# A transformer block on one Trainium2 core: weight bounds from sums on ScalarE, filler products on TensorE, a planner with longer transfer estimates, and part of h transposed by DMA

## The chip, the cores and the metric

The kernel runs on one core of one Trainium2 chip. Its engines are TensorE (PE in the profile, its weight loads PEld), VectorE (DVE), ScalarE (ACT), GpSimd (POOL) and SyncE (SP), which here only issues transfers; a second queue of transfers is issued by ScalarE (ACTq). The metric is the device time of one execution in microseconds. The kernel before takes 1078.31 us, the median of three runs (1075.23 to 1079.66).

## The reference

```python
B, S, D = 1, 2048, 640;  H = 32; Dh = 20; W = 256;  F = 1536
qkv = layernorm(x) @ wqkv                                # no scale or shift in the norm
scores = einsum("bhqd,bhkd->bhqk", q, k) * Dh ** -0.5
mask = (i - j >= 0) & (i - j < W)                        # a sliding window of 256 keys
o = softmax(where(mask, scores, -1e9)) @ v
h = x + o @ wo
h2 = h + (gelu(layernorm(h) @ w_gate) * (layernorm(h) @ w_up)) @ w_down
```

All inputs and the output are 32-bit floats.

## The kernel before

**Tiles.** The 2048 rows are 16 blocks of 128. q and k are made for chunks of two blocks (`qk`, eight chunks), v for one block (`vproj`), the feed-forward for chunks of four blocks (`gate_up`, `down`, four chunks of three weight groups each). Every dense product is made of three 16-bit products: each operand is split into a high half (`...h`) and a low half (`...l`), and hi*hi, hi*lo and lo*hi are summed in a PSUM bank. So 75 matmuls of 256 columns make q (or k) of a chunk.

**Weights.** `Weight.scale` finds a power of two that brings a weight into range: DVE takes the largest absolute value of each of its five slices of 128x640 (tile `am`), a small product with a diagonal (`dg`) spreads it over the partitions, and a few short DVE operations make the scale `sw`. `Weight.split` then makes the high half on ACT and the low half on DVE. The weights are numbered in the profile: w0 is q's, w1 k's, w2 v's, w3 that of the output product, gu and w5 to w9 gate and up, w10 to w12 down.

**Attention.** For each block and each pair of heads there are two short row-tiled products, each on two halves of the array at once: `maxima` (q times k, whose row maxima DVE takes in `max_out`, tile `junk`) and, once a block's maxima have gone through `max_rows` and a transfer into two spare rows of qT, `scores` (k times q, exponentiated by ACT in `score_out` into `pt`, masked by GpSimd). Four score tiles make a unit, which `value_lane` multiplies with v (tile `pv`). q and k reach their stacked layout through DRAM: `qk_out` writes 16-bit halves from the ACT queue and `stack` reads them back with six transfers each from the SP queue into `qT` and `kT`.

**Layer norms.** `layernorm` normalises a block on DVE (tile `lxn` for h) with one power on GpSimd, and `transpose_part` transposes it on TensorE in two pieces of four and one 128x128 tiles into the bank `tp`; ACT casts the high half out of PSUM and DVE subtracts the low half. The first chunk of h is normalised during attention (`first_norm_lane`), the other three are read back from DRAM in the feed-forward (`chunk_lane`, `norm_lane`, tiles `hTh` and `hTl`).

**What sets the order.** The program is written out by a planner. Each task is a generator (a lane) that says for which engine and operands it waits; class `Clock` keeps an estimated time of every engine and operand, and the loop at the end takes the first lane in a list of priorities that its estimate lets start now. What comes out is a fixed order on each engine. On the chip an engine carries out its row in that order, and waits only for semaphores. `row_need` chooses whether the two banks of `ra` and `rb` hold a maxima and a scores pair next; `Lane.start` holds the allowances.

The names and lines that the prediction speaks of are `Clock.issue` (158), `Weight.scale` (352) and `split` (387), `layernorm` (422), `stack` (664), `maxima` (719), `row_need` (739), `scores` (823), `norm_lane` (1064) and `big_lane` (543).

## Time and profile before

| | |
|---|---|
| median of three runs | 1078.31 us (1075.23 to 1079.66) |
| profiled execution, its own time | 1078.47 us |
| profiled execution, span | 1076.6 us |
| TensorE busy | 1031.5 us (96%) |
| VectorE, ScalarE, GpSimd busy | 673.8, 456.8, 182.8 us |
| mean granted TensorE clock | 0.994 |

The profile's page shows a single execution. The busy time of TensorE counts a matmul from its start to its modelled end, so successive matmuls overlap in it; what a matmul costs is the distance to the start of the next one. In the timeline, each row has a start, the time from the first start to the last end of the merged instructions, the engine, the operation, out<-in, shapes and a count; what stands in brackets is the time that the engine sat idle before it and what ended that. Nearly every instruction is recorded in a helper and so has the line L188: groups are told apart by their tiles. DMA issues on SP and ACT are rows of SPq and ACTq, and last as long as the issue, not the transfer.

### The profile page before, as it was taken

How to read it: one execution, taken by the hardware profiler on the slowest of the kernel's cores; microseconds unless marked ns; L12 is line 12 of the kernel's file. 1: busy time of each engine (PE TensorE's matmuls, PEld its weight loads, DVE VectorE, ACT ScalarE, POOL GpSimd, SP SyncE). 2: the span in 40 equal slices, each digit the busy share in tenths (PEclk: the TensorE clock that was granted, in tenths of full speed). 3: DMA queues.
4: the chain of work that ended last, by engine and by line, in shares of the span. 5: the costliest groups of instructions: out<-in, count | busy, mean ns of one | idle time of the engine just before them, and what ended most of it. 6: DMA issues, size and time to landing. Idle time of an engine off the chain costs nothing.

```text
span 1076.6 us, 25043 instructions
## 1 busy us (share of the span) xinstructions
PE 1031.5 (96%) x10122; PEld 632.3 (59%) x10122; DVE 673.8 (63%) x1993; ACT 456.8 (42%) x904; POOL 182.8 (17%) x297
## 2 busy tenths in 40 slices
PE   4888899999999999999999999999999999999998
PEld 2645566666776666676655564555555555545546
DVE  7967799888778777776789379724522262212323
ACT  2414466665676666665667744310211121110110
POOL 5001113232333333332333300000000000000000
PEclk9989999999999999999999999999999999999999
DMA  7536436214142230414142034002000020001001
GB/s 280 124 93 161 141 108 169 85 58 116 38 113 63 74 88 30 105 57 98 32 173 65 13 122 147 2 1 98 1 1 1 25 74 1 1 1 50 1 1 49
DMA packets 63251, 76.91 MB, mean 71 GB/s; under 512 B 6112, under 2 KB 42208, under 8 KB 62176
## 3 DMA queue, kind: packets, MB, share of 16 engines
q1 hardware_dynamic: 40032, 64.57, 20.2%
q10 hardware_dynamic: 23104, 10.75, 3.7%
q8 instruction: 79, 1.29, 0.5%
q14 instruction: 36, 0.29, 0.1%
HBM read 54.07 MB, written 20.97 MB: 70 GB/s over the span
## 4 chain that ended last, share of the span: by engine, by line
PE 82%; DVE 8%; DMA 3%; ACT 3%; issue 2%; ACTq 1%; POOL 0%; SPq 0%; DVEq 0%; POOLq 0%
PE mm L188 62%; PE pv L188 7%; PE tp L188 4%; PE ra L188 4%; PE rb L188 4%; DVE junk L188 2%; ACT pt L188 2%; DVE am L188 1%; DMA qk<-qks 1%; DMA kT<-qk 1%; ACTq L188 1%; DMA wsl<-in_wo_dram 1%; DVE m L188 1%; DMA qT<-in_wqkv_dram 1%; DMA xt<-in_x_dram 1%
## 5 line engine op out<-in xcount | busy, mean ns | idle before, releaser
L188 POOL TENSOR_SCALAR_AFFINE_SELECT pt<-pt 128x512 f32<-128x512 f32 x240 | 151.0, 652 | 371.6 <-ACT pt L188 371.6
L188 ACT ACTIVATE pt<-ra,esc 128x384 f32<-128x384 f32 (+2 forms) x262 | 133.0, 560 | 82.9 <-PE ra L188 71.4
L188 DVE CUSTOM_DVE_ANT_0 junk<-rb,mask 128x384 bf16<-128x384 f32 (+2 forms) x260 | 138.1, 531 | 44.1 <-PE rb L188 23.4
L188 DVE CUSTOM_DVE_ANT_0 junk<-ra,mask 128x384 bf16<-128x384 f32 (+2 forms) x252 | 133.0, 528 | 43.5 <-PE ra L188 19.5
L188 ACT ACTIVATE pt<-rb,esc 128x384 f32<-128x384 f32 (+2 forms) x250 | 126.9, 561 | 71.0 <-PE rb L188 64.3
L188 DVE SCALAR_TENSOR_TENSOR gel<-mm,ffk,gel 128x512 f32<-128x512 f32 x48 | 35.9, 749 | 141.4 <-PE mm L188 141.4
L188 ACT ACTIVATE gel<-mm,ffk 128x512 f32<-128x512 f32 x48 | 33.0, 688 | 187.9 <-PE mm L188 187.8
L188 PE MATMUL pv<-pt,v 128*21 128x128 f32 x2880 | 104.3, 276 | 1.7 <-ACT oT L188 1.5
L188 DVE SCALAR_TENSOR_TENSOR ht<-mm,ffk,ht 128x320 f32<-128x320 f32 x96 | 52.8, 550 | 81.6 <-PE mm L188 81.6
L188 PEld LDWEIGHTS <-ah 128*128 128x128 f16 x768 | 75.1, 98 | 30.9 <-issue 0.4
L188 ACT CAST ah<-gel 128x512 f16<-128x512 f32 x48 | 29.8, 621 | 121.2 <-DVE gel L188 121.1
L188 PEld LDWEIGHTS pv<-pt,v 128*21 128x21 f32 x2880 | 68.6, 100 | 16.7 <-ACT oT L188 2.2
L188 PEld LDWEIGHTS <-gu 128*128 128x128 f16 x480 | 45.8, 98 | 53.0 <-issue 0.8
L188 PEld LDWEIGHTS <-kT 62*128 62x128 f16 x1440 | 59.2, 94 | 28.0 <-issue 14.2
L188 PE MATMUL mm<-hTh,gu 128*128 128x512 f16 x240 | 71.9, 379 | 0.0
L188 PEld LDWEIGHTS <-qT 60*128 60x128 f16 x640 | 26.3, 93 | 70.2 <-issue 65.2
L188 PE MATMUL mm<-xh,w1h 128*128 128x256 f16 x200 | 55.6, 278 | 3.0 <-DVE qks L188 3.0
L188 PE MATMUL mm<-xh,w0h 128*128 128x256 f16 x200 | 56.1, 280 | 1.9 <-ACT w0h L188 1.9
L188 PE MATMUL mm<-xh,w0l 128*128 128x256 f16 x200 | 55.7, 278 | 1.0 <-DVE w0l L188 1.0
L188 PE MATMUL mm<-xh,w1l 128*128 128x256 f16 x200 | 55.8, 279 | 0.2 <-DVE w1l L188 0.2
L188 PE MATMUL mm<-xl,w0h 128*128 128x256 f16 x200 | 55.9, 280 | 0.0
L188 PE MATMUL mm<-xl,w1h 128*128 128x256 f16 x200 | 55.6, 278 | 0.0
(214 smaller groups left out, 2316.2 us busy)
## 6 DMA issues: line engine op xcount, KB each, us to landing
qk<-qks ACTq DMA_DIRECT2D x64, 128.0 KB
qT<-qk SPq DMA_DIRECT2D x48, 160.0 KB
kT<-qk SPq DMA_DIRECT2D x48, 160.0 KB
ht<-in_x_dram SPq DMA_DIRECT2D x16, 320.0 KB
h_dram<-ht SPq DMA_DIRECT2D x16, 320.0 KB
ht<-h_dram SPq DMA_DIRECT2D x16, 320.0 KB
out_dram<-ht SPq DMA_DIRECT2D x15, 320.0 KB
xt<-in_x_dram SPq DMA_DIRECT2D x13, 320.0 KB
```

The source lines that it names most:

```text
L188: r = real(*args, **kw)
```

## The change

Four things are changed.

1. **Bounds from sums.** For the three weights of q, k and v, `scale` takes the sum of absolute values of each slice on ACT (an `Abs` activation with `accum_out`) in place of the largest absolute value on DVE. The sum bounds the maximum, so the power of two is larger. The output of the activation goes into the room of the high half, which is written anew by `split`.
2. **Filler products.** As long as no maxima have been issued, whenever the planner finds nothing to do and TensorE free in its estimate, it writes a product of the 16-bit identity with itself into the order (into `pv`).
3. **Planner.** A transfer is estimated to land 2.6 us (SP) or 2.2 us (other queues) after its bytes in place of 1.7, its issue to take 0.7 us where its rows are short, and its bytes 1.2 times as long. Transfers of `stack` are spaced by that estimate. Lanes marked `soon` (short links of a chain) come first. Blocks 0 and 1 put two pairs of heads into a bank (`pairs`). `row_need` may also choose two scores or two maxima pairs. The memsets of `kT` on GpSimd wait until w0 is scaled. GELU and `down` wait until their scales have been written.
4. **h of chunks 1 to 3.** `turned` casts the normalised block to a high half on ACT (tile `sph`, 128x640), subtracts the low half on DVE (`spl`), and two transposing transfers on the SP queue write them into `hTh` and `hTl`. The twelve blocks are no longer transposed on TensorE and nothing of them goes through PSUM.

The core of the diff:

```diff
@@ Clock.issue, Engine
         if move:
-            self.t[eng] = start + 0.4
-            self.moved[eng] = max(self.moved[eng], start + 0.2) + cost
-            end = self.moved[eng] + 1.7
+            run = min(b[4] for a, (_, b) in zip(reads + writes, boxes[0] + boxes[1])
+                      if a.space != DRAM)
+            self.t[eng] = start + (move if run > 512 else 0.7)
+            self.moved[eng] = max(self.moved[eng], start + 0.2) + cost * (1.2 if run <= 512 else 1)
+            end = self.moved[eng] + (2.6 if eng == "sync" else 2.2)
...
+                             {"dma_start": 0.4, "dma_start_transpose": 1.2}.get(op))
@@ Weight.scale
             for i in range(n):
+                if self.hl:
+                    yield on("scalar", self.raw[0, i])
+                    nc.scalar.activation(self.hl[0][:, i, :], self.raw[0, i], AF.Abs,
+                                         accum_out=am[:, i:i + 1])
+                    continue
@@ layernorm, after xn is made
+        if dma:
+            yield from turned(xn, lane, (hi, lo), dst, when)
+            return
...
+    def turned(src, lane, to, dst=None, when=None):
+        yield on("scalar", src, when=lambda: not opened["parts"] and (not when or when()))
+        opened["parts"] += 1
+        hi, lo = (nc.tile(ffp, [P, D], F16, n) for n in ("sph", "spl"))
+        nc.scalar.copy(hi, src)
+        yield on("vector", hi)
+        nc.vector.tensor_tensor(lo, src, hi, op=ALU.subtract)
+        if dst:
+            to = dst()
+        for o, i in zip(to, (hi, lo)):
+            yield ("sync",), need(i, eng="sync")
+            nc.sync.dma_start_transpose(o, i)
+        opened["parts"] -= 1
@@ big_lane
-                yield on("gpsimd")
+                yield on("gpsimd", when=lambda: W["q"].scaled)
@@ stack
+                if c > 1:
+                    yield ("sync",), lambda: nc.moved["sync"] - PACE
@@ pairs, used by maxima, scores, max_out and score_out
+    def pairs(j):
+        return 2 if j < 2 else 1
@@ row_need
+        late = max(ta, nc.t["tensor"]) + APART
+        two_of = [(maxima, scores, tm[:1] + ts[:1]), (scores, scores, ts), (maxima, maxima, tm)]
+        if lead > LEAD + SWAY:
+            two_of = [two_of[1], two_of[0], two_of[2]]
+        elif lead < LEAD - SWAY:
+            two_of = [two_of[2], two_of[0], two_of[1]]
+        for f, g, t in two_of:
+            if len(t) == 2 and max(tb, *t) <= late:
+                row.extend([(f, a), (g, b_)])
+                return max(tb, *t)
@@ gelu, down
-        yield on("scalar", ps)
+        yield on("scalar", ps, when=lambda: pos["ffk", fg])
...
-        yield pe(when=lambda: w.ready and pos["act", c, fg] == FT)
+        yield pe(when=lambda: w.ready and w.down and pos["act", c, fg] == FT)
@@ norm_lane
-                                 xn=lambda: nc.tile(ffp, [P, D], F32, "lxn", 2))
+                                 xn=lambda: nc.tile(ffp, [P, D], F32, "lxn", 2), dma=True)
@@ the loop at the end
+        first = [l for l in trans + sides if isinstance(l.engs, Soon)]
-        order = (early + outs + trans + sides
+        order = (first + early + outs + trans + sides
...
         else:
+            if not pos["max"] and nc.t["tensor"] <= now:
+                nc.tensor.matmul(pv[:, 0, :], ident16, ident16, start=True, stop=True)
             now += 0.03
```

How the rows of three engines move. First ScalarE at the start of the program, before: the four casts belong to the transposes of x blocks 0 and 1, `w0h<-qT,sw` is the split of q's weight, whose slices lie in the tile qT at first.

```order
L188 ACT_TABLE_LOAD
L188 CAST xh<-tp 128x4x128
L188 CAST xh<-tp 128x128
L188 CAST xh<-rb 128x4x128
L188 CAST xh<-rb 128x128
L188 ACTIVATE w0h<-qT,sw 128x640 x5
L188 ACTIVATE qks<-mm 128x512
```

And now:

```order
L190 ACT_TABLE_LOAD
L190 ACTIVATE w0h,am_159<-qT 128x640 x2
L190 CAST xh<-tp 128x4x128
L190 ACTIVATE w0h,am_159<-qT 128x640
L190 CAST xh<-rb 128x4x128
L190 ACTIVATE w0h,am_159<-qT 128x640
L190 CAST xh<-tp 128x128
L190 CAST xh<-rb 128x128
L190 ACTIVATE w0h,am_159<-qT 128x640
L190 ACTIVATE w1h,am_349<-gu 128x640 x2
L190 ACTIVATE w0h<-qT,sw 128x640 x5
```

The five sums of w0 (those with `am`) now stand on ScalarE between the casts, and the third, fourth and fifth of them stand behind casts that need TensorE's transposes.

TensorE at its first transposes, before and then now (`ident_76` is the 16-bit identity; 52 rows of the filler product stand ahead of the piece shown):

```order
L188 MATMUL tp<-ident,xt 128x128 x5
L188 MATMUL rb<-ident,pt 128x128 x4
L188 MATMUL ra<-dg,ones 128x128
L188 MATMUL rb<-ident,pt 128x128
L188 LDWEIGHTS w0h
L188 MATMUL mm<-xh,w0h 128x256
```

```order
L190 LDWEIGHTS ident_76
L190 MATMUL pv<-ident_76 128x128
L190 MATMUL tp<-ident,xt 128x128 x4
L190 LDWEIGHTS ident_76
L190 MATMUL pv<-ident_76 128x128
```

The first five transposes stood at the head of the row; now a run of filler products precedes them, and further runs (14, 7, 4 and 38 products) stand between them and the small product with `dg` that spreads the bound of w0. 247 filler products are in the program in all.

SyncE's queue from the last weight to the results of the first feed-forward chunk, before and then now:

```order
L188 DMA wst<-in_wd_dram 128x640 x4
L188 DMA ht<-h_dram 128x640 x4
L188 DMA out_dram<-ht 128x640 x4
L188 DMA ht<-h_dram 128x640 x4
```

```order
L190 DMA wst<-in_wd_dram 128x640 x4
L190 DMA ht<-h_dram 128x640 x4
L190 DMA_TRANSPOSE hTh<-sph 128x5x128
L190 DMA_TRANSPOSE hTl<-spl 128x5x128
L190 DMA_TRANSPOSE hTh<-sph 128x5x128
L190 DMA_TRANSPOSE hTl<-spl 128x5x128
L190 DMA_TRANSPOSE hTh<-sph 128x5x128
L190 DMA_TRANSPOSE hTl<-spl 128x5x128
L190 DMA_TRANSPOSE hTh<-sph 128x5x128
L190 DMA_TRANSPOSE hTl<-spl 128x5x128
L190 DMA out_dram<-ht 128x640 x4
```

Eight transposing transfers stand between the loads of a chunk of h and the stores of the chunk before it. On TensorE the 60 transposes `tp<-ident,lxn` of chunks 1 to 3 are gone (384 transposes into `tp` before, 324 now). Over the whole program TensorE goes 282 times into a run of the row-tiled products of attention before, and 252 times now.

More of the change, by code (lines that the diff above doesn't have):

```diff
@@ L156, in others, with issue @@
                             if e != eng])
-    def issue(self, eng, cost, reads, writes, move=False):
+    def issue(self, eng, cost, reads, writes, move=None):
         start = self.t[eng]
@@ L192, in call @@
                 out, ins = [aps[0], aps[-1]], aps[1:-1]
+            if "accum_out" in kw:
+                out, ins = [aps[0], aps[-1]], aps[1:-1]
             if op in ("memset", "affine_select"):
                 ins = out if op == "affine_select" else []
-            self.clock.issue(self.name, self.cost(op, out[0], ins), ins, out, op == "dma_start")
+            self.clock.issue(self.name, self.cost(op, out[0], ins), ins, out,
+                             {"dma_start": 0.4, "dma_start_transpose": 1.2}.get(op))
             return r
@@ L385, in scale, with room @@
             self.known = True
+        def room(self, pool):
+            if not self.hl:
+                self.hl = pool if isinstance(pool, tuple) else [
+                    nc.tile(pool, [P] + self.shape, F16, f"w{self.col}{x}") for x in "hl"]
         def split(self, pool, spread=0):
-            self.hl = pool if isinstance(pool, tuple) else [
-                nc.tile(pool, [P] + self.shape, F16, f"w{self.col}{x}") for x in "hl"]
+            self.room(pool)
+            self.begun = True
             sc = sw[:, self.col:self.col + 1]
@@ L682, in stack @@
             for b in (2 * c, 2 * c + 1):
-                for pr in range(H // 2):
+                for pr in range(0, H // 2, pairs(b)):
                     heapq.heappush(maxq, (b, pr))
@@ L750, in row_need @@
+        free = 3 - (pos["units"] - pos["values"])
+        for j, pr in list(scoreq)[:2]:
             b = B[j]
-            ts = nc.ready((b.c.qT[0:62, pr, b.cols], b.c.qT[64:126, pr, b.cols]), "tensor")
-            if pr % 2 == 0 and pos["units"] - pos["values"] >= 3:
-                ts = INF
+            free -= pr % 2 == 0
+            if free >= 0:
+                ts.append(nc.ready((b.c.qT[0:62, pr, b.cols], b.c.qT[64:126, pr, b.cols]),
+                                   "tensor"))
         row.clear()
-        both = tm is not None and ts is not None
@@ L756, in row_need @@
-        lead = pos["max"] - pos["score"]
-        if both and max(tb, tm, ts) > max(ta, nc.t["tensor"]) + APART:
-            both = False
-            if max(tm, ta) > max(ts, ta) + APART or lead > LEAD and ts < INF:
-                tm = None
-            else:
-                ts = None
-        if both:
-            row.extend([(maxima, a), (scores, b_)])
-            return max(tb, tm, ts)
-        if tm is not None:
-            row.append((maxima, a))
-            return max(ta, tm)
-        if ts is not None:
-            row.append((scores, a))
-            return max(ta, ts)
@@ L774, in block_kernel @@
+        one = [(max(ta, t[0]), f) for f, t in ((maxima, tm), (scores, ts)) if t]
+        if len(one) == 2:
+            (t0, _), (t1, _) = one
+            one = one[1:] if t0 > t1 + APART or lead > LEAD else one[:1]
+        if not one:
+            return INF
+        row.append((one[0][1], a))
+        return one[0][0]
     row = []
@@ L820, in max_transpose @@
         side.append((LATE, residual(j)))
-        scoreq.extend((j, pr) for pr in range(H // 2))
+        scoreq.extend((j, pr) for pr in range(0, H // 2, pairs(j)))
     def scores(at_):
@@ L1154, in dense_lane @@
                 else:
-                    yield pe(when=lambda: woq or any(can(*t) for t in list(todo)[:AHEADQ]))
+                    yield pe(when=lambda: woq and W["o", 0].ready
+                             or any(can(*t) for t in list(todo)[:AHEADQ]))
             else:
```

112 lines of the change are left out of this document (67 added, 45 removed).

## The prediction

> **What bounds the kernel now.** I read the page first, then a table of five stretches.
>
> ```profile
> span 1076.6 us, 25043 instructions
> PE 1031.5 (96%) x10122; PEld 632.3 (59%) x10122; DVE 673.8 (63%) x1993; ACT 456.8 (42%) x904; POOL 182.8 (17%) x297
> PE 82%; DVE 8%; DMA 3%; ACT 3%; issue 2%; ACTq 1%; POOL 0%; SPq 0%; DVEq 0%; POOLq 0%
> core 0: us, PE busy (x) PEld busy (x) DVE busy (x) ACT busy (x) POOL busy (x), PEclk, DMA share, GB/s
> 0.00:58.00 58.00, 33.45 (x232) 24.20 (x232) 47.73 (x123) 20.38 (x35) 17.10 (x31) 0.99 0.65 198
> 58.00:120.00 62.00, 54.26 (x454) 34.14 (x456) 45.01 (x189) 19.83 (x50) 5.57 (x9) 0.90 0.51 141
> 120.00:620.00 500.00, 490.57 (x6875) 321.56 (x6869) 394.38 (x1293) 329.46 (x676) 153.28 (x245) 1.00 0.30 83
> 620.00:1073.00 453.00, 452.98 (x2569) 252.38 (x2567) 186.13 (x388) 87.10 (x143) 6.86 (x12) 1.00 0.10 33
> ```
>
> TensorE carries 82% of the chain, but not equally. From 620 us on it never stops, so there only fewer matmuls help. From 120 to 620 us it idles 9.4 us, but pays for going to and fro between dense and row-tiled products. Up to 120 us it idles 32.3 us (24.55 and 7.74); in the second stretch the clock of 0.90 takes another 62 * 0.10 = 6.2 us. What is to be gained lies at the start, in the changes to and fro, and in the transposes of the end.
>
> **The transposes of chunks 1 to 3.** TensorE in the feed-forward:
>
> ```profile
> 753.03 0.38 PE L188 MATMUL mm<-hTh,w5l 128*128 128x512 f16 x1
> 753.25 0.60 PE L188 MATMUL tp<-ident,lxn 128*128 128x128 f32 x4
> 753.69 0.38 PE L188 MATMUL mm<-hTh,w5h 128*128 128x512 f16 x1
> 753.90 0.38 PE L188 MATMUL mm<-hTl,w5h 128*128 128x512 f16 x1
> ```
>
> Four transposes push the next matmul back from 753.25 to 753.69, 0.11 us each. Sixty are removed: 6.6 us on the path. In their place ACT casts 640 columns once rather than 512 and 128, and DVE subtracts once rather than twice, both with more than half their time free there (87 and 186 of 453 us). The transfers are new; they cost nothing if they land in time.
>
> ```profile
> 675.57 0.60 DVE L188 TENSOR_SCALAR lxn<-ht,lmvi,lyi 128x640 f32<-128x640 f32 x1
> L188 PE MATMUL mm<-hTh,gu x80: 379/379/379, 705.2 to 730.9; 128*128 128x512 f16 x80
> 46.82 4.94 SPq L188 DMA_DIRECT2D kT<-qk  x6
> 54.08 0.21 PE L188 MATMUL ra<-kT,qT 60*128 60x128 f16 x1 [0.74 <-DMA kT<-qk]
> q1 hardware_dynamic: 40032, 64.57, 20.2%
> ```
>
> Chunk 1 is the tight one: its first blocks are normalised by 676 us, cast by 677, and TensorE wants them at 705.2, less the 2.2 us that its own 20 transposes no longer take: 703. Eight transfers of 160 KB stand in one queue. If each takes T and the last needs 2.3 us to be seen (54.08 less the end of issue at 51.76), they fit while T is below (703 - 677 - 2.3) / 8 = 3.0 us. The trace shows no transposing transfer. Low end: the six kT transfers, of the same size, 0.82 us each. High ends: a packet on this queue takes 20.2% of 16 * 1076.6 us / 40032 = 87 ns; a tile moved in 640 packets of 256 bytes over 16 engines takes 3.5 us, in 32-byte pieces eight times that. I take 1 to 2 us, near the kT row, since both put short rows into SBUF; so 6.6 us are gained whole. Behind them in SP's row wait only the stores of the finished chunk and the next loads of h, which are used 117 us later (three groups of 120 * 0.216 and 96 * 0.136 us). ACT's third cast waits for the first pair to leave its two buffers; GELU stands behind it.
>
> The Trainium skill speaks against this part: VectorE: DVE Perf Modes, section The three transpose paths, has a 128x128 tile at 390 ns on TensorE and 1309 ns by transposing DMA, and advises TensorE where PSUM will do. By that figure T would be an estimated 6.5 us for five tiles in turn, which is the first rival below. The trace has TensorE at 0.11 us rather than 0.39, and nothing on the other figure.
>
> **The start, 0 to 58 us.**
>
> ```profile
> 7.21 0.82 DVE L188 TENSOR_REDUCE am<-qT 128x1 f32<-128x640 f32 x1 [0.84 <-DMA qT<-in_wqkv_dram]
> 10.60 1.09 PE L188 MATMUL tp<-ident,xt 128*128 128x128 f32 x4 [10.60 <-DVE xt L188]
> 11.72 0.59 ACT L188 CAST xh<-tp 128x512 f16<-128x512 f32 x1 [9.64 <-PE tp L188]
> 17.48 3.70 ACT L188 ACTIVATE w0h<-qT,sw 128x640 f16<-128x640 f32 x5 [0.76 <-DVE sw L188]
> 25.24 0.42 PE L188 MATMUL mm<-xh,w0h 128*128 128x256 f16 x1
> 25.45 0.34 PE L188 MATMUL mm<-xl,w0h 128*128 128x256 f16 x1
> 25.73 0.27 PE L188 MATMUL mm<-xh,w0h 128*128 128x256 f16 x1
> 26.89 1.10 ACTq L188 DMA_DIRECT2D qk<-qks  x2
> 31.09 0.27 PE L188 MATMUL mm<-xh,w0l 128*128 128x256 f16 x1
> 43.89 0.27 PE L188 MATMUL mm<-xh,w1l 128*128 128x256 f16 x1
> 58.27 0.26 PE L188 MATMUL ra<-kT,qT 60*128 60x128 f16 x1 [3.98 <-DMA xt<-in_x_dram]
> ```
>
> DVE is the engine in demand (47.7 of 58 us), and until 25.4 us TensorE runs at half rate: a product of 256 columns every 0.21 us, then every 0.109. The sums take 15 reductions of 0.8 us off DVE and put them on ACT, at 0.83 us each by the split's row. This does not bring w0 forward. The filler needs the 16-bit identity, whose cast stands on DVE behind the statistics of x block 1 (done at 6.1 us here), so 52 products at 0.107 us (half of 0.21) run from 6.5 to 12 us and the first transposes follow at 12, not 10.6. ACT's third sum stands behind their cast: sums three to five, with casts of 0.6, 0.6 and two of 0.3 us between them, end near 17, `sw` follows at 18.8 and w0h 1.3 us later than before. But TensorE is then warm: 15 products are through when the last low half comes at 23.7, the other 60 take 6.5 us, with a wait for a bank q is done near 31, as before. k gains: its sums end at 25.1, its split runs on ACT from 27.1 to 33.4, k is done at 42 in place of 44. Then ACT is short: from 27 to 54 us it has ten splits and five more sums (12.4 us), four times 1.5 us of `qks`, eight casts (3.4) and 24 issues of some 0.5, altogether 34 us of work. So banks come free late and I put the first maxima at 57.7. By then TensorE has done 75 + 75 + 75 + 30 products, 27.8 us of work. Before, it had done 150 of these and 50 of 320 columns (0.136 us), 23.2 us, at 58.3, and came out of a wait of 4 us at half clock, which cost 2.4. The gain is 4.6 + 0.6 + 2.4, say 7 us. Bounds: 13 if ACT delays nobody, a loss of 4 if it is 11 us later still.
>
> **Waits from 58 to 120 us.**
>
> ```profile
> 86.75 0.23 PE L188 MATMUL rb<-qT,kT 62*128 62x128 f16 x1 [2.96 <-DMA qT<-mT]
> 113.79 0.47 PE L188 MATMUL ra<-qT,kT 62*128 62x128 f16 x2 [3.23 <-ACT pt L188]
> 116.23 0.42 PE L188 MATMUL mm<-xh,w1h 128*128 128x256 f16 x1
> ```
>
> Idle time and clock cost 7.7 + 6.2 us here; 2.4 are counted above, 11.5 remain. After a wait of 3 us products come every 0.21 us again, for 3.4 us by the clock, so such a wait costs 2.96 + 1.7 = 4.7 us. The first of the two is TensorE at the first scores, for the maxima that ACT sends back into qT. It stays, I think: 27 dense products stood between the transpose of block 0's maxima and these scores, 31 stand there now, 0.4 us more for a way that lacked 3 us; ACT's row is not shorter, and the filler has ended with the first maxima. The second wait, and small ones, lie where transfers estimated 0.5 to 0.9 us later give another order. Of their 11.5 - 4.7 = 6.8 us I take half, 3.5; bounds 11.5, and a loss of 3 for a wait elsewhere.
>
> **Changes to and fro.**
>
> ```profile
> 99.14 0.27 PE L188 MATMUL mm<-xl,w0h 128*128 128x256 f16 x1
> 99.35 0.28 PE L188 MATMUL rb<-kT,qT 60*128 60x256 f16 x2
> 99.47 0.22 PE L188 MATMUL ra<-qT,kT 62*128 62x128 f16 x2
> 99.62 0.28 PE L188 MATMUL mm<-xh,w0l 128*128 128x256 f16 x1
> ```
>
> From 99.14 to 99.62 are 0.48 us, while the streams need 0.109 + 0.107 + 0.053 = 0.27: a trip costs 0.21 us. There are 252 in place of 282: 6 us. Bounds 10 (trips that also carry v cost more) and nothing. The 9.4 us of idle time up to 620 us I leave as they are: two maxima pairs at once ask four reductions of DVE in a row, two scores pairs four exponentials of ACT, and the banks come free later; the later transfers save some waits. The bounds are 6 us better and 8 us worse.
>
> **The sum.** 6.6 + 7 + 3.5 + 6 = 23.1 us, span 1053.5; the profiled execution took 1078.47 us, 1.9 over its span and within 0.2 of the median 1078.31. Forecast 1055 us, chance 0.57 for 1045 to 1066.
>
> **Rivals.**
>
> 1. *Slow transposes, slower than before.* The place is the first product of chunk 1 at 703 us. Above T = 3.0 us it waits 8 * (T - 3.0) us, once; chunks 2 and 3 have some 65 us (normalised around 753, wanted at 820), which hold up to T = 8. The gain of 23 us is used up at T = 3.0 + 23 / 8 = 5.9; at 8 us the time is 1055 + 40 = 1095. For it: pieces under 256 bytes would be far over 8 us, and the same queue has carried nothing of the kind. Against: the kT row, short rows of the same size at 0.82 us. Chance 0.09. By the skill's figure above, T = 6.5 would give 1055 + 28 = 1083.
> 2. *Only the transposes count.* The start gains nothing because ACT, with 34 us of work in 27, takes DVE's place; first maxima come after 62 us, and new waits eat what the trips give: 1078.3 - 6.6 = 1072. For it: ACT's rows, which now hold sums, splits, casts and issues one behind the other. Against: TensorE's clock, which the filler holds while it waits. Chance 0.19.
> 3. *All waits go.* The ends of the bounds, 13 + 11.5 + 10 + 6.6 = 41 us: 1037. For it: every wait quoted is for a transfer or ACT, whose estimates are what changes. Against: 31 products in place of 27 at the first scores. Chance 0.15.
>
> **How the numbers follow.** A measurement of this kernel can tell about 0.5% (5.4 us) from no change. Faster means below 1072.9: the forecast, the third rival and half of the second, 0.57 + 0.15 + 0.09 = 0.81. The same: the other half and the first rival with T near 6, 0.12. Slower: 0.07. The range 1035 to 1075 takes in the second rival and most of the third and leaves out about 0.2, more of it above than below.
>
> **What would show it.** `tp<-ident,lxn` left with 20 matmuls; no TensorE wait for hTh or hTl near 703; transposing transfers of 1 to 2 us. PEclk at 1.0 from 13 us on; first `w0h<-qT,sw` at 18.8, first maxima at 57.7, ACT the fullest engine beside TensorE in between. A TensorE wait of some 3 us at the first scores, with the clock at half behind it, would confirm the part that I leave. A wait at chunk 1 would show the first rival, first maxima after 62 us the second, a 120 to 620 us stage that idles well over 9.4 us that the trips bought nothing. The forecast is wrong as a whole if the start is no shorter although the filler runs.

## The result

The kernel after takes 1072.20 us, the median of eight runs (1069.13 to 1075.74), against 1078.61 for eight runs of the kernel before (1075.23 to 1081.68). The ratio is 0.9939 with a 95% interval of 0.9919 to 0.9959: 6.4 us less, where 23 were forecast. The profiled execution took 1069.6 us, 1.9 over its span and 2.6 below the median.

The page of the kernel after, span, busy times and the first line of the chain of waits:

```profile
span 1067.7 us, 25424 instructions
PE 1034.6 (97%) x10309; PEld 642.1 (60%) x10309; DVE 660.0 (62%) x1966; ACT 459.2 (43%) x890; POOL 184.4 (17%) x297
...
PE 79%; DVE 12%; DMA 3%; issue 3%; ACT 2%; POOL 0%; ACTq 0%; DVEq 0%; SPq 0%; POOLq 0%
```

VectorE's share of the chain went up from 8% to 12%, though it has less to do in all. The same stretches as in the prediction, and the 30 us from 120 on by themselves:

```profile
0.00:58.00 58.00, 48.50 (x534) 44.03 (x534) 38.66 (x109) 32.06 (x66) 16.92 (x31) 1.00 0.67 205
58.00:120.00 62.00, 56.51 (x479) 37.21 (x480) 48.40 (x208) 15.38 (x37) 5.13 (x8) 0.94 0.45 118
120.00:150.00 30.00, 25.07 (x305) 13.89 (x304) 24.44 (x75) 18.83 (x35) 7.46 (x11) 0.83 0.45 119
120.00:620.00 500.00, 485.38 (x6808) 317.50 (x6807) 388.73 (x1276) 326.07 (x658) 155.05 (x247) 0.99 0.32 85
620.00:1073.00 453.00, 444.24 (x2491) 243.42 (x2490) 184.19 (x375) 85.71 (x131) 7.29 (x12) 1.00 0.15 43
```

And before, the same 30 us:

```profile
120.00:150.00 30.00, 29.79 (x332) 19.71 (x325) 26.78 (x95) 18.51 (x46) 5.57 (x9) 1.00 0.30 87
```

The start did get shorter. But from 120 to 150 us TensorE was busy for 29.79 us at a clock of 1.00 before; now it is for 25.07 at 0.83, and from 120 to 620 us it idles 14.6 us (500 - 485.38) rather than 9.4. (The last row reaches beyond the end of this execution, at 1067.7; TensorE stops at 1064.3, and before that its time is full.)

Busy time holds neither the trips nor the half clock. So I worked a second measure out of the trace. Each product of TensorE is counted at the distance at which its kind follows in an undisturbed stream (0.109 us for 256 columns, 0.136 for 320, 0.216 for 512, 0.107 for a 32-bit transpose, the filler at nothing). A short tiled product counts as its share of such a stream, some 0.027 us for 128 columns. What is left of a stretch is *lost*: waits, trips, half clock, filler. All figures of this kind come from the one profiled execution of a kernel, whose time can lie several us from the kernel's median (1075.8 against 1081.2 for e2 below), so differences of 2 or 3 us between kernels say little. "Lead" below is how much more of this streamed work a kernel has done than the kernel before at the same moment.

| us | streamed in all | lost 0-120 | lost 120-150 | 150-200 | 200-500 | 500-620 | lost 120-620 |
|---|---|---|---|---|---|---|---|
| before | 925.8 | 55.1 | 4.4 | 10.1 | 55.4 | 21.9 | 91.8 |
| after | 919.4 | 42.9 | 15.8 | 7.6 | 53.7 | 24.6 | 101.7 |

The three differences (-6.4, -12.2 and +9.9) make -8.7 us, and the spans differ by 8.9 (1076.6 - 1067.7): beyond 620 us nothing else changed. In leads: 12.2 us at 120, 0.8 at 150, 2.3 at 620. The start's gain was real, and was handed back within 30 us.

**Where it was handed back.** TensorE around 125 us, after:

```profile
125.84 0.30 PE L190 MATMUL mm<-w2h,xl 128*128 128x320 f16 x1
...
127.47 0.32 PE L190 MATMUL ra<-kT,qT 60*128 60x384 f16 x1 [0.49 <-ACT pt L190]
...
136.09 0.38 PE L190 MATMUL rb<-qT,kT 62*128 62x128 f16 x7 [0.49 <-DVE mxs L190]
...
138.18 0.32 PE L190 MATMUL ra<-kT,qT 60*128 60x384 f16 x1 [0.39 <-DVE mxs L190]
...
142.32 0.45 PE L190 MATMUL mm<-w3h,oh 128*128 128x320 f16 x1
```

Dense products (`mm`) fill TensorE's time while DVE and ACT work through the maxima and the scores. The last one that was ready is v's at 125.84; the next, the output product of block 0, comes at 142.32. In between stand maxima, scores, values and a few transposes, many of them behind a bank that DVE or ACT has yet to empty.

The dense products ran out because x came late, and DVE's row shows why. After, the last reduction of block 0's maxima, the step that gathers them, and the statistics of x block 6:

```profile
75.84 0.29 DVE L190 CUSTOM_DVE_ANT_0 junk<-ra,mask 128x128 bf16<-128x128 f32 x1
...
76.28 0.42 DVE L190 CUSTOM_DVE_ANT_0 junk<-rb,mask 128x256 bf16<-128x256 f32 x1
...
95.95 0.56 DVE L190 CUSTOM_DVE_ANT_0 junk<-ra,mask 128x384 bf16<-128x384 f32 x1
...
96.43 0.18 DVE L190 TENSOR_SCALAR m<-mxs 128x32 f16<-128x32 f32 x1
...
104.14 0.48 DVE L190 BATCH_NORM_STATS2 lstx<-xt 128x6 f32<-128x320 f32 x1
...
130.69 0.92 DVE L190 TENSOR_SCALAR xt<-xt,lmvx,lyx 128x640 f32<-128x640 f32 x1
```

Before:

```profile
74.60 0.29 DVE L188 CUSTOM_DVE_ANT_0 junk<-rb,mask 128x128 bf16<-128x128 f32 x1
...
78.74 0.18 DVE L188 TENSOR_SCALAR m<-mxs 128x32 f16<-128x32 f32 x1
...
92.06 0.61 DVE L188 TENSOR_SCALAR xt<-xt,lmvx,lyx 128x640 f32<-128x640 f32 x1
...
113.16 0.61 DVE L188 TENSOR_SCALAR xt<-xt,lmvx,lyx 128x640 f32<-128x640 f32 x1
```

The maxima of two pairs in each bank (`pairs`) put reductions into DVE's row four at a time. Before, six reductions of block 1 stood between block 0's last and its gathering step; now 36 do, and it runs at 96.43 rather than 78.74. So the first scores come at 102.40 us rather than 83.58. The first output product is only 2.8 us later than before (139.55 there), so it isn't what filled the same stretch before. X blocks 6 and 7 are normalised at 107.08 and 130.69 rather than 92.06 and 113.16 (the load of block 7 is issued only at 103.95, when DVE has come to the statistics of block 6; before, at 63.62), so chunk 3 of q and k is late, and with it the dense products that would come next.

### The profile page after: what moved, and what is told of

It reads as the page before. It is cut to its first block, busy times and chain, and to the rows that moved or that the text cites. A ratio compares the mean times of both kernels' runs of the same rounds, so it can differ in the third digit from the quotient of the medians.

```text
span 1067.7 us, 25424 instructions
## 1 busy us (share of the span) xinstructions
PE 1034.6 (97%) x10309; PEld 642.1 (60%) x10309; DVE 660.0 (62%) x1966; ACT 459.2 (43%) x890; POOL 184.4 (17%) x297
## 4 chain that ended last, share of the span: by engine, by line
PE 79%; DVE 12%; DMA 3%; issue 3%; ACT 2%; POOL 0%; ACTq 0%; DVEq 0%; SPq 0%; POOLq 0%
PE mm L190 61%; PE pv L190 8%; DVE junk L190 6%; PE ra L190 4%; PE rb L190 4%; PE tp L190 4%; DMA qk<-qks 1%; ACT pt L190 1%; DMA kT<-qk 1%; DVE am L190 1%; DVE m L190 1%; DMA wsl<-in_wo_dram 0%; DMA qT<-mT 0%; DVE o L190 0%; DVE xt L190 0%
## 5 line engine op out<-in xcount | busy, mean ns | idle before, releaser
L190 ACT ACTIVATE pt<-ra,esc 128x384 f32<-128x384 f32 (+2 forms) x242 | 127.5, 579 | 73.4 <-PE ra L190 55.4
```

What stands on the lines that cost most here:

```text
L190: r = real(*args, **kw)
```

## Experiments

All ratios are to the kernel before, run on the same chip in the same hour, with 95% intervals; us are that ratio times 1078.6. Diffs are against the kernel after unless said otherwise.

### The transposes alone, and all but the transposes

`e1_dma_only` is the kernel before with `turned` and `dma=True` and nothing else of the change. `e2_no_dma`:

```diff
-                                 xn=lambda: nc.tile(ffp, [P, D], F32, "lxn", 2), dma=True)
+                                 xn=lambda: nc.tile(ffp, [P, D], F32, "lxn", 2))
```

> The kernel before with one part of the change: h of chunks 1 to 3 by transposing DMAs; every other row stands as before. Theory A (the transposes are about all that the change gains, since what the start wins is handed back by 148 us): 60 transposes of 0.107 us fall away, -6.4 us, 1072 us, as fast as the whole change. Theory B (the rest of the change brings what was forecast, and the transposes bring less): 1078, no gain.

> The changed kernel without the transposing DMAs: TensorE transposes h of chunks 1 to 3 again, the other parts stay. Theory A: 1072.2 + 6.4 = 1078.6 us, no better than the kernel before. Theory B: 1072, the other parts hold the gain.

Measured: e1 0.9914 (0.9893 to 0.9936), 1069.3 us; e2 1.0005 (0.9978 to 1.0032), 1079.1 us. The transposes by themselves bring as much as the whole change, and the rest of it brings nothing that these runs can tell from zero. In e2 the start is won (44.0 us lost up to 120) and handed back (98.7 from 120 to 620, against 91.8).

The kernel after by tiles: the transposes that are left on TensorE, and its products on the transposed h (count, then the duration in ns, then the first and the last start):

```profile
L190 PE MATMUL tp<-ident,lxn x20: 272/273/329, 177.1 to 273.6; 128*128 128x128 f32 x20
...
L190 PE MATMUL mm<-hTh,gu x240: 379/379/379, 700.6 to 960.0; 128*128 128x512 f16 x120
```

Its timeline on SP, the first and the last of chunk 1's eight transfers:

```profile
674.69 1.33 SPq L190 DMA_TRANSPOSE hTh<-sph  x1
...
693.28 1.23 SPq L190 DMA_TRANSPOSE hTl<-spl  x1
```

And the transfers between 674 and 696 us, by queue (packets, MB, share of the 16 engines):

```profile
q1 hardware_dynamic: 5376, 1.31, 36.1%
```

Twenty transposes are left of 80. All eight transfers are issued by 694.5 us, and TensorE's first product on them starts at 700.6 behind no wait. 1.31 MB in 5376 packets are 244 bytes each; a transfer of 160 KB makes 640 packets of 256 bytes, and the trace has 32 of 4 bytes beside each. 36.1% of 22 us is 7.9 us for the eight transfers, 1 us each; one that runs alone moves from 680.43 to 681.37, in 0.95 us.

### The filler

```diff
             if not pos["max"] and nc.t["tensor"] <= now:
-                nc.tensor.matmul(pv[:, 0, :], ident16, ident16, start=True, stop=True)
+                nc.issue("tensor", nc.tensor.cost("matmul", pv[:, 0, :], [ident16, ident16]),
+                         [ident16, ident16], [pv[:, 0, :]])
```

`e3_no_fill` leaves out the 247 filler products; the planner still counts their time, so the order of everything else is unchanged (in the traces too).

> The changed kernel without its 247 small products on the identity; every other instruction stands in the same order. TensorE's clock should be half until about 23 us and again in the waits before 60 us, which costs 3 to 5 us by 60 us. Theory A (a delay before 120 us is taken up by the dry stretch of 126 to 148 us, where TensorE waits for the attention rows and has no dense products): under 1 us of it is left at the end, 1072 to 1073 us. Theory B (delays of the start go through to the end): 1075 to 1077 us.

Measured: 0.9899 (0.9870 to 0.9928), 1067.7 us. The filler earns nothing: 44.3 us are lost up to 120 without it, 42.9 with it, and afterwards 101.7 either way. In two more pairs of kernels without and with it (e11 and e6, e7 and e4, below) the one without was ahead by 3.0 and 3.6 us. TensorE's first rows after show a price:

```profile
6.27 5.11 PE L190 MATMUL pv<-ident 128*128 128x128 f16 x52 [6.27 <-DVE ident L190]
...
16.46 3.29 PE L190 MATMUL pv<-ident 128*128 128x128 f16 x56
...
19.59 0.27 PE L190 MATMUL mm<-xh,w0h 128*128 128x256 f16 x1
```

The 52 fillers ahead of the first transposes hold up ACT's casts and the sums behind them, so that w0h is split from 17.43 on rather than from 14.75 in e3; then the last run of 56 stands ahead of the first product of q. It comes at 19.59, without the fillers at 15.6. The filler does keep the clock at 1.00 from 10.6 to 58 us, but no time saved by that is in the result.

### The dry stretch from 120 to 150 us

`e4_x_first` lets the lanes of x go first, and start later in the planner's estimate, from the first maxima until block 7 is normalised:

```diff
+    def hurry():
+        return pos["max"] and not B[7].ready
...
-                back = EARLY if not B[XF].ready else LATE
+                back = EARLY if not B[XF].ready else OUT + 0.1 if hurry() else LATE
...
-        early = [l for l in sides if l.gen.__name__ == "x_lane"] if not B[XF].ready else []
+        early = [l for l in sides if l.gen.__name__ == "x_lane"] if not B[XF].ready or hurry() else []
```

> The changed kernel with one rule more: from the first maxima until block 7 is normalised, the lanes that load and normalise x go ahead of all others. Theory A (dense products run out at 126 us because x of block 7 is loaded at 104 us and normalised at 131, behind maxima and weight slices): the stretch of 120 to 150 us loses 5 us of TensorE and not 16, and the time falls by 8 to 11 us to 1061 to 1064. Theory B (the attention rows set the end of the stage at 613 us whatever the dense products do): 1071 to 1073 us.

`e13_m_soon` lets the gathering step of the maxima go ahead of other work on DVE; `e14_m_x` is both:

```diff
-        yield on("vector", when=lambda: j < 2 or B[j - 2].turned)
+        yield soon("vector", when=lambda: j < 2 or B[j - 2].turned)
```

> The changed kernel with one condition of the planner's changed: the step that turns a block's maxima into the negated 16-bit pair may go ahead of other work on DVE, as the steps behind it may already. In the changed kernel block 0's step stands behind all 64 reductions of blocks 0 and 1 and runs at 96.4 us, though its own 32 were done at 76; in the kernel before it ran at 78.7. Now it stands behind 34. Theory A (this is what takes the start's lead back: the first scores come at 102 and not at 84 us, so block 0's output and the products with wo that would fill the dry stretch come late): first scores near 84 us, the dry stretch under half its length, 1060 to 1065 us. Theory B (only the late x of block 7 matters for the dry stretch): first scores near 84 us, but TensorE runs dry from 126 to 148 as before, 1069 to 1073.

> That step ahead, and x of blocks 6 and 7 first as well. Both products that can fill the stretch, wo's and q's, are then early. Theory A: 1056 to 1062 us, with at most 6 us lost from 120 to 150. Theory B: as with x first alone, 1064 to 1068.

Measured: e4 0.9877 (0.9847 to 0.9907), 1065.3 us; e13 0.9911 (0.9882 to 0.9939), 1069.0; e14 0.9903 (0.9874 to 0.9932), 1068.1. The stretch itself, in e4, e13 and e14:

```profile
120.00:150.00 30.00, 29.63 (x368) 19.47 (x367) 26.51 (x84) 19.99 (x39) 8.31 (x13) 0.97 0.39 108
```

```profile
120.00:150.00 30.00, 25.32 (x253) 13.79 (x250) 26.19 (x88) 12.35 (x26) 5.75 (x9) 0.89 0.55 132
```

```profile
120.00:150.00 30.00, 30.00 (x337) 21.11 (x333) 27.93 (x96) 13.03 (x26) 3.69 (x6) 1.00 0.51 145
200.00:500.00 300.00, 287.63 (x4122) 191.47 (x4120) 219.94 (x750) 188.46 (x383) 91.17 (x149) 0.98 0.28 70
```

Early x is enough to fill the stretch: e4 loses 6 us there rather than 15.8, though it pays 5.6 us of the start's gain for that. Early scores are not: e13 has its first scores at 82.0 us and the stretch stays at 25.32. Both together fill it wholly (e14), and this is the run that teaches most. At 200 us e14 leads the kernel before by 16.2 us, about what the forecast had for start, waits and trips together; at 500 it leads by 2.3. TensorE then idles 12.4 us between 200 and 500 (6.25 before), with a dry stretch of its own from 314 to 322 us and two waits for kT of 3.6 and 3.5 us; and the clock of 0.98 takes another 6 us, where it was 1.00 before. The two make up most of the 13.9 us of lead that are lost there. So filling the stretch is not enough. The lead moves on and is lost at the next place where dense products run out.

### v before q and k of chunk 1

`e6_v_first` puts the v products of blocks 0 and 1 ahead of q and k of chunk 1 in the list of dense work (`can` and the choice among the first of the list as before, but only the head while that is one of these two). The planner then puts in 338 filler products in place of 247:

```diff
         for c in range(NC2 + 1):
+            if c == 1:
+                todo.extend([(vproj, 0), (vproj, 1)])
             if c < NC2:
                 todo.extend([(qk, c, 0), (qk, c, 1)])
-            if c:
+            if c > 1:
                 todo.extend([(vproj, 2 * c - 2), (vproj, 2 * c - 1)])
```

> The changed kernel with v of chunk 0 ahead of q and k of chunk 1 in the list of dense products. In the changed kernel the six loads of kT of chunk 0 go 2 us apart and the first maxima wait 5.1 us for them. Theory A (each of those loads waits for a completion counter that a store of q of chunk 1 holds): with v ahead no such store is about, the loads go 0.8 us apart as before, the wait at the first maxima is under 2 us and they end by 57 us; TensorE idles or turns on the identity 2 to 3 us before v. At the end within 3 us of the changed kernel, since x of block 7 is still late (normalised behind 68 to 78 reductions). Theory B (the loads are slow because the transfers are): the loads go 2 us apart again and the wait stays.

Measured: 0.9837 (0.9805 to 0.9869), 1061.0 us, 11 us better than the change. SP's issues of kT and the wait at the first maxima, in the timelines after and then in e6:

```profile
46.33 9.52 SPq L190 DMA_DIRECT2D kT<-qk  x6
...
60.40 0.37 PE L190 MATMUL rb<-kT,qT 60*128 60x128 f16 x3 [5.14 <-DMA kT<-qk]
```

```profile
43.51 6.04 SPq L190 DMA_DIRECT2D kT<-qk  x6
...
55.22 0.27 PE L190 MATMUL rb<-kT,qT 60*128 60x128 f16 x3 [0.83 <-issue]
```

Six loads that take 6 us to issue in e6 take 9.5 after. The program deals eight completion counters out to all transfers in turn, and in the kernel after three of the six loads (the third, fourth and sixth) wait on SP for the store of q of chunk 1 that last used theirs. With v first, these stores come later in the program. The trace after bears this out: each of the three loads waits on the counter that it then uses itself, and starts (50.79, 52.75 and 55.10) right when the store that used it last (issued at 47.38, 49.77 and 51.08) is seen to have landed. The gaps before them, 1.5, 1.2 and 0.8 us, are the 3.5 us of difference. No run changed the counters alone, so what this wait costs at the end is not shown. What e6 gains at the start is small besides (42.2 us lost up to 120, against 42.9). It loses 94.5 us from 120 to 620, against 101.7, and that is its gain: v is there early, so the dry stretch has dense products (5 us lost from 120 to 150, against 15.8). The expectation was right on the loads and wrong on the end, where it had no gain over 3 us.

Four kernels combine these edits: `e7_x_first_no_fill` is e4 and e3, `e8_x_v_first` adds e6 to that, `e11_v_first_no_fill` is e6 and e3, and `e15_m_v_no_fill` adds e13 to that. `e12_v_first_x9` is e6 with the x lanes of blocks 8 and 9 first (`hurry` returns `B[7].ready and not B[9].ready`).

> The changed kernel with x of blocks 6 and 7 first, and without the 247 small products (nothing else moved by that). Theory A (the small products are worth nothing, they hold up w0's first products by 4 us): as fast as with x first alone or up to 3 us faster, 1063 to 1067. Theory B (now that the start's gain is kept, the clock they hold is worth 3 us): 1069 to 1071.

> x of blocks 6 and 7 first, v of chunk 0 ahead of q and k of chunk 1, no small products. If both delays add: 1060 to 1064. If the attention stage is bound at its end whatever is won ahead of it: 1065 to 1067, as with x first alone.

> v of chunk 0 ahead of q and k of chunk 1, and none of the small products; nothing else moved. With v first TensorE waits some 3 us for w2 and again for kT, so a clock at half could cost: by the clock's row, 3.4 us at half after each wait. If the small products hold the clock to some use: 1064 to 1066. If they only delay w0's first products, as without v first: 1060 to 1062.

> That step ahead, v of chunk 0 ahead of q and k of chunk 1, no small products: the fastest combination so far (1060) and the step. If the two delays add: 1054 to 1058. If the late scores were covered there already (first scores at 91 us): 1059 to 1062.

> v of chunk 0 ahead of q and k of chunk 1, and x of blocks 8 and 9 ahead of other work once block 7 is done. With v first alone TensorE loses 17 us from 150 to 200 us, with q of the fifth chunk waiting for block 9, normalised at 180 us. Theory A (every dry stretch comes from x that is late): that stretch loses 9 to 12 us, 1055 to 1059 in all. Theory B (what is won before 200 us is lost by 620): 1061 to 1063.

Measured: e7 0.9843 (0.9813 to 0.9873), 1061.7 us; e8 0.9847 (0.9810 to 0.9883), 1062.1; e11 0.9809 (0.9782 to 0.9837), 1058.0; e15 0.9838 (0.9798 to 0.9877), 1061.1; e12 0.9991 (0.9975 to 1.0008), 1077.6. Nothing adds up. e4 and e6 are worth 7 and 11 us alone and 10 together, without the filler (e8). e12, meant to cure the next dry stretch, gives 17 us back: from 200 to 250 and from 500 to 560 us it loses some 20 us each, where e6 loses some 10. Neither expectation of e12 allowed for that.

### The other parts of the change, undone one by one

`e5_old_rows` has the rule of before in `row_need` and one pair in each bank (`pairs` returns 1). `e9_old_estimates`:

```diff
-            self.t[eng] = start + (move if run > 512 else 0.7)
-            self.moved[eng] = max(self.moved[eng], start + 0.2) + cost * (1.2 if run <= 512 else 1)
-            end = self.moved[eng] + (2.6 if eng == "sync" else 2.2)
+            self.t[eng] = start + 0.4
+            self.moved[eng] = max(self.moved[eng], start + 0.2) + cost
+            end = self.moved[eng] + 1.7
```

`e10_max_on_dve` takes the maxima of all three weights on DVE again, with no sums on ACT, and `e16_m_max_dve` is e13 and e10:

```diff
         W[n].load(rooms[n])
-        W[n].room(wq)
```

> The changed kernel with the rule for the attention rows of before: maxima and scores go in turn, one pair each, and none covers two head pairs. In its order the statistics of x block 6 stand behind 14 maxima reductions again and not behind 74, and block 7's load ahead of the weight slices. Theory A (the dry stretch comes from the maxima, two pairs at once, that keep DVE from normalising blocks 6 and 7; the fewer trips are worth about 6 us from 150 to 400 us): 120 to 150 us wastes 5 us and not 16, 150 to 400 us wastes 47 us as before and not 41; together 1064 to 1070 us. Theory B (the trips saved are the only gain of the middle, the dry stretch has another cause): the dry stretch stays and the time rises by 4 to 6 us to 1076 to 1078.

> The changed kernel with the transfer estimates of before: 0.4 us of an engine for each and 1.7 us to the landing, with nothing added for short rows. The loads of kT and q of chunk 1 are planned earlier, but block 6 of x is still behind 70 maxima or so. Theory A (the parts of the change beside the transposes have no worth of their own; what counts is whether dense products run out, and that has its cause in the order of DVE and of the transfers): the same as the changed kernel, 1068 to 1074 us, with a dry stretch near 130 us. Theory B (the later estimates remove waits, as forecast with 3.5 us): 1075 to 1077.

> The changed kernel with the bounds of the three first weights from maxima on DVE again. DVE gets 12 us of reductions back before 45 us and ACT loses 12.5. Theory A (DVE is the engine in demand at the start, the sums save it work and bring k and v forward; but the lead is paid back in the dry stretch): first maxima 2 to 6 us later, the end 0 to 3 us later, 1071 to 1075. Theory B (the start's lead goes through): 4 to 7 us later, 1076 to 1079.

> That step ahead, and the first weights' bounds from maxima on DVE again. With maxima on DVE alone 1062 us was measured, 10 us less than with ScalarE's sums, while TensorE ran dry at 126 us all the same; where that gain comes from is open. If it is the start on ACT (34 us of work in 27): both gains add, 1053 to 1059. If it is only another order of the later rows: 1060 to 1070.

Measured: e5 0.9905 (0.9870 to 0.9941), 1068.4 us; e9 0.9868 (0.9825 to 0.9912), 1064.4; e10 0.9827 (0.9802 to 0.9852), 1059.9; e16 0.9767 (0.9737 to 0.9798), 1053.5. So none of these three parts earns its place in this program: with each undone, the kernel is no slower, and with the sums undone 12 us faster, where both expectations had it slower. e5 gives up the whole gain up to 120 us (55.1 lost, as before), makes 282 trips again, and is still no slower. In e5 and e9 the stretch from 120 to 150 us isn't dry any more (5 and 7 us lost); for e9 the dry stretch was expected to stay. e16 is the fastest of all: a median of 1054.64 us (1053.46 to 1056.42), ahead of both kernels. It has what the forecast had for the whole change, without the sums: 11.7 us less lost up to 120, 5.0 after that, and 6.4 of transposes.

Of the parts undone, only the row rule with its pairs carries the start's gain. From 58 to 120 us the kernel before loses 24 us, the kernel after 16, e9 17 and e10 14, but e5 25. That stretch in e5 and in e10:

```profile
58.00:120.00 62.00, 55.71 (x446) 30.59 (x447) 49.43 (x207) 23.09 (x61) 6.80 (x11) 0.82 0.56 139
```

```profile
58.00:120.00 62.00, 57.99 (x511) 37.91 (x509) 50.38 (x216) 15.41 (x35) 4.30 (x7) 0.97 0.45 120
```

Where e10 and e16 gain: a row of the kernel after, then two of e10 and two of e16:

```profile
500.00:620.00 120.00, 115.78 (x1584) 67.16 (x1583) 87.62 (x266) 82.15 (x163) 40.55 (x62) 1.00 0.23 70
```

```profile
120.00:150.00 30.00, 25.61 (x325) 15.00 (x324) 26.88 (x86) 20.39 (x40) 8.79 (x13) 0.89 0.45 130
500.00:620.00 120.00, 118.70 (x1550) 70.81 (x1545) 79.83 (x234) 83.51 (x166) 35.32 (x58) 1.00 0.20 65
```

```profile
120.00:150.00 30.00, 27.79 (x319) 15.41 (x318) 27.05 (x89) 19.19 (x37) 6.74 (x10) 1.00 0.42 112
200.00:500.00 300.00, 296.63 (x4321) 202.42 (x4318) 233.14 (x794) 196.74 (x399) 92.63 (x151) 1.00 0.33 83
```

From 120 to 150 us e10 is as dry as the change (25.61 at a clock of 0.89), from 500 to 620 it idles 1.3 us rather than 4.2. e16 keeps the full clock in the first of these, and idles 3.4 us from 200 to 500. The sums concern the first 60 us, yet at 120 and at 150 us e10 has the lead of the change (11.3 and 0.9 us against 12.2 and 0.8); the gain arises from 200 us on (50.6 lost up to 500 against 53.7, and 18.1 up to 620 against 24.6). A shift in the first 60 us gives the planner another order for all that follows, and more filler products (363 in e10 and e16, against 247), which no run took out. Which property of that order gains is not settled. The clock is part of it: from 120 to 620 us it is at half for 13.6 us in the profiled execution after, which costs some half of that, 6.8 us; for none in e9, e15 and e16; for 20.5 us in e12.

### Changes that mean nothing

The planner's clock goes on in steps of 0.03 us where nothing can start. `e17_step_29` and `e18_step_31` make this 0.029 and 0.031: but for one filler product more (248), only the order shifts.

> The changed kernel with one number changed that means nothing for the chip: the planner's clock goes forward in steps of 0.029 us in place of 0.030 when nothing can be issued. What each instruction does is the same; some 1300 TensorE instructions from the first stretch on stand in another order. Theory A (each part of the change won or lost by the order into which the planner fell, not by what it does): the time differs from the changed kernel by 3 to 10 us, to either side. Theory B (the parts have prices of their own, and orders of this kind are worth alike): 1071 to 1073 us.

> The same with steps of 0.031 us. Theory A: it differs from the changed kernel by 3 to 10 us, and from the run with 0.029 too. Theory B: 1071 to 1073 us.

Measured: e17 0.9955 (0.9935 to 0.9976), 1073.7 us; e18 0.9968 (0.9947 to 0.9989), 1075.1. They are 1.7 and 3.1 us above the change, between the two expectations, and single stretches move by more: e18 loses 61.4 us from 200 to 500 where the change loses 53.7. Effects of 3 or 4 us (e5, e13, e14) can therefore not be told from a shift of the order. e3 has the order of the kernel after, so a shift is not its cause, but its 4 us are hardly clear of the two intervals; that all three pairs agree is what speaks against the filler. The effects of e6, e10 and e16 (11 to 18 us) are well beyond what the two shifts did, and of the other sign; those of e4 and e9 (7 and 8 us) less clearly, as the four runs of e9 range from 1061.85 to 1070.91. Two such kernels don't bound how far an order can wander.

All kernels in the two stretches that matter:

| lost us | 0-120 | 120-620 | | 0-120 | 120-620 |
|---|---|---|---|---|---|
| before | 55.1 | 91.8 | e9 old estimates | 44.3 | 92.2 |
| after | 42.9 | 101.7 | e10 maxima on DVE | 43.8 | 93.3 |
| e1 DMA only | 53.8 | 91.8 | e11 v first, no filler | 42.5 | 92.8 |
| e2 no DMA | 44.0 | 98.7 | e12 v first, x 8 and 9 | 46.2 | 108.8 |
| e3 no filler | 44.3 | 101.7 | e13 m soon | 39.6 | 100.5 |
| e4 x first | 48.5 | 93.9 | e14 m soon, x first | 40.9 | 103.0 |
| e5 old rows | 55.1 | 90.5 | e15 m soon, v first, no filler | 42.3 | 91.0 |
| e6 v first | 42.2 | 94.5 | e16 m soon, maxima on DVE | 43.4 | 86.8 |
| e7 x first, no filler | 46.0 | 92.4 | e17 step 0.029 | 45.7 | 104.8 |
| e8 x and v first, no filler | 46.0 | 94.9 | e18 step 0.031 | 42.5 | 108.8 |

Apart from e1 and e5, every kernel keeps half or more of the start's gain. What separates these, from e16 at 1054 to e12 at 1078 us, is mostly the second column.

## Why the prediction was right or wrong

**The transposes: right.** 6.6 us were forecast. The streamed work fell by 6.4, e1 gave 9.3 and e2 took away 7.1, each uncertain by some 2 to 4 us. T is 0.95 us of moving and 1.20 of issue, in the range of 1 to 2 that the kT row gave, so the first rival has no ground. The Trainium skill (VectorE: DVE Perf Modes, The three transpose paths) has 1309 ns for a 128x128 tile by DMA, and its Rules for kernel authors prefer TensorE where PSUM will do. The trace has five such tiles moved in 0.95 us, and e2, which transposes on TensorE, is 7 us slower.

**The start: the number right, the reasons mostly not.** 7 + 3.5 us up to 120 were forecast, 12.2 measured; that they agree is in good part luck. Up to 58 us 5 were gained rather than 7, and from 58 to 120 us 7.5 rather than 3.5. The filler, the sums and the estimates, to which the forecast owed both terms, can each be undone and the gain stays (e3, e10 and e9 lose 44.3, 43.8 and 44.3 up to 120); with the row rule and the pairs, which it did not count here, it goes (e5, 55.1). The steps fell near where they were put: w0h's split at 17.43 (18.8), q done at 30.0 (31), k at 41.1 (42), first maxima at 55.05 (57.7). Then TensorE waited 5.14 us for kT, which the prediction did not have, and the 3-us wait at the first scores did not come, as these came 19 us later than before. The second rival named the right time, 1072, and that new waits eat what is won, but for a wrong reason: ACT did not hold the start up. From 27 to 54 us it was busy for 15.8 us beside its issues, DVE for 22.5, where the prediction had ACT the fuller with 34 us of work; and the sums, put at 0.83 us each, came every 0.72 us (the split's row itself gives 3.70 / 5 = 0.74).

**The filler: wrong.** The prediction gave the warm clock some 2.4 us of the start, and spoke for the filler against the second rival. Without it e3 keeps the start (44.3 against 42.9) and is 4 us faster in the end.

**The trips: wrong.** 30 fewer were to save 6 us. They were 252 as forecast, but e5, with 282, is no slower. (e5 changes what DVE has to do as well, so the price of a trip by itself is not isolated.) From 200 to 400 us the kernels after and before make nearly the same number (95 and 96), so the saved ones lie near the two ends of attention. Dense products are short there, and a trip saved may only lengthen a wait; that is argued, not shown.

**The step that failed** is the term for 120 to 620 us: "The 9.4 us of idle time up to 620 us I leave as they are", with the bounds of 6 better and 8 worse, no cost at all for a half clock there, and under it the assumption that a lead won by 120 us lasts to the end. TensorE idled 14.6 us, 5.2 more, which the bounds allow. But it also ran at half clock for 13.6 us, 130.0 to 133.4, 140.2 to 147.0 and, about a wait of 2.59 us for kT, 450.9 to 454.3; that costs some 6.8 us, and before there was none:

```profile
450.90:454.30 3.40, 2.93 (x17) 1.72 (x18) 0.57 (x2) 1.05 (x2) 0.00 (x0) 0.50 0.00 0
```

Together these are 12.0 us. What is left of the lost time, in which the trips are, fell by 2.1 us (9.9 - 12.0) and not by 6. The prediction named the mechanism of the dry stretch itself (two maxima pairs ask four reductions of DVE in a row) and looked only at the banks, not at what stands behind 36 reductions on DVE: the gathering step, the statistics of x and with them the load of the next block, and through x the dense products that were missing from 125 to 142 us. The stretch from 120 to 620 was forecast to lose 6 us less and lost 9.9 more. These 15.9 us, less the 1.7 by which the start did better than 10.5, are the 14.2 us by which the forecast span, 1053.5, missed the measured 1067.7. Whether a lead lasts hangs on the order: even with the gathering step and x mended it did not in e14, nor in e12 and e18, while e9, e10, e11, e15 and e16 hand back 2 us or nothing of theirs.

**Open:** which property of an order makes it good from 200 us on; why the maxima on DVE help there; how much of e6's gain is the counters; which of the two edits of e5 takes the start away. The lanes marked `soon`, the spacing of `stack`, the memsets and the waits of GELU and `down` were not undone alone. From 519 to 546 us the kernel after has only 60 dense products (8 us of streamed work), half of them v of block 15, which the program lets wait for a buffer of the ring of v; a larger ring was not tried.

## What to carry to other kernels

Where a planner writes one order for all engines, a faster start is only a lead, which some orders keep and others lose: ask for each engine what stands behind the work that is now packed together, and whether the stream that fills the waits (here the dense products, fed by x) comes forward with it. Measure each part alone, and beside it one change that means nothing, to see how far the order wanders by itself: filler, sums and planner looked like gains on paper, and undoing any one of them made the kernel no slower. Transposes of a bound TensorE are worth handing to the DMA where the result has time to land; here 6 us between the end of the last issue and the first use were enough.

## What the runs showed of the hardware

- A transposing transfer of 128x640 16-bit elements out of SBUF took 1.2 us of its queue's issue in the median (1.96 at most) and moved in 0.95 us, in 640 packets of 256 bytes and 32 of 4. Eight of them made 5376 packets and took 7.9 us of 16 engines: 24 ns a packet on each, not the 87 of the queue's mean before.
- The granted clock fell to half behind stretches in which TensorE was busy for some 70% of the time (2.67 of 4 us, 4.70 of 6.6), though it never stood still for long. The kernel after, in consecutive pieces of the dry stretch (the third column from the end is the clock):

```profile
126.00:130.00 4.00, 2.67 (x39) 1.26 (x38) 3.68 (x13) 3.39 (x6) 1.27 (x2) 1.00 0.24 71
130.00:133.40 3.40, 3.37 (x37) 2.04 (x38) 3.26 (x9) 2.03 (x4) 1.48 (x2) 0.50 0.28 81
133.40:140.00 6.60, 4.70 (x82) 2.72 (x77) 5.79 (x20) 4.34 (x8) 1.27 (x2) 1.00 0.42 122
140.20:147.00 6.80, 6.60 (x63) 3.32 (x60) 4.87 (x17) 3.27 (x6) 1.88 (x3) 0.51 0.55 133
```

  No single wait in these pieces is longer than 0.5 us. By the clock's share the two pieces at half cost some 5 us (half of 3.4 and of 6.8), a third of the 15.8 lost from 120 to 150, beside 4.9 us of idle time: here many small waits cost more than their sum. The Trainium skill (TensorE: Matmul & The Clock Gate, Part 1: The HAM clock gate) has the clock fall after an idle window of some 3.4 us. The two pieces at half, of 3.4 and 6.8 us, agree with such a window; that it must be idle, these rows do not bear out.
- Executions of one and the same kernel differ in their mean granted clock, and their times with it: of e9's four one took 1061.85 us at 0.997 and one 1070.91 us at 0.989. By the clock, 0.008 of some 1066 us, that is 8.5 us; the times differ by 9.1.
- Loads on one queue were held up by stores on another with which they share a completion counter: six loads took 9.52 us to issue rather than 6.04, and the 3.5 us between are three waits for such counters (not changed alone in any run).
